# Two expert networks behind windowed attention: where the second sums accumulate, and when prepared weight slices are stored

## The chip, the cores and the metric

The kernel runs on one core of one Trainium2 chip. The metric is the device time of one execution in microseconds (us), as the median of several runs; less is better. TensorE (PE, with its weight loads as PEld) multiplies, VectorE (DVE) and ScalarE (ACT) do elementwise work, the queue of SyncE (SP) issues nearly all transfers, and the kernel's matmul results land in eight banks of PSUM.

## What is computed

The reference is attention over windows of chunks of 32 queries, with eight memory slots, followed by two feed-forward networks on 3072 tokens with 512 channels and 2048 hidden columns:

```python
for c in range(nc):                       # chunk 32, left 16, right 8, 8 memory slots
    a = softmax(scale * q_c @ k_full.T)   # k_full, v_full: memory and window
    out[:, :, c_start:c_end] = a @ v_full
x = out.transpose(0, 2, 1, 3).reshape(B * S, H * D)
r = np.maximum(x @ w_in1, 0.0)
x = (s * (r * r) + b) @ w_out1            # first network
h = x @ w_in2
out = (h * (1.0 / (1.0 + np.exp(-1.702 * h)))) @ w_out2   # second network
```

## The kernel before

**Arithmetic.** Each fp32 operand is split into a high and a low part (names ending in h and l), and each product of 128x128 by 128x512 is three matmuls: high by high, high by low, low by high. Tokens are cut into six blocks of 512. The hidden columns are cut into sixteen slices j of 128.

**Stages.** Attention of 24 tiles of 128 tokens runs beside the first network. Blocks 0 to 3 of the first network go through 66 units (`step`): a unit is one slice j for one block, four hidden sums into a bank of the ring `h`, four gate steps on ACT and DVE, and four output sums into `accA` and `accB` (two banks each). Each weight slice is loaded, taken apart on ACT and DVE (`words`, `prep`) in a ring `st` of three buffers and a ring `u` of four, and then stays in SBUF; all 32 are prepared in the first 150 us.

**Sweeps of seven products.** Blocks 4 and 5 of the first network, and then all six blocks of the second network in pairs, are done by `seven(s)`: for a pair of blocks (bp, bq) and a pair of slices, seven half-sized matrix products stand in for eight. A sweep takes eight steps p. The products accumulate in four places: A and C, one bank each of the ring `h` (two banks), B and D, the two banks of the tile `a`. DVE combines them in the SBUF tile `ys` (spots 0 to 3). The gates of block bp are used at once: `out_of(bp, ...)` adds them into `accA` (k = 0, 1) and `accB` (k = 2, 3) between the products; this is the first sum. The gates of block bq are stored to DRAM (`gd`), but for those of the last step, which stay in SBUF (`gq`). After step 7 and the last two `out_of(bp, ...)`, the sixteen `out_of(bq, ...)` follow; this is the second sum, 16 times 12 matmuls. It too accumulates in `accA` and `accB`, which `finish` has to copy out (`evac`, L223) first. Slices 14 and 15 come first from `gq`; the other fourteen are read back (`again`, L1136), the even ones into the ring `g`, the odd ones into the tile `back`, which takes the place of `ys`. During the second sum of the first sweep the output weights of the second network are also loaded (`reload`, L850), 512 KB a slice.

**The prepared slices.** `combine(p)` makes, for the sweep of the first network, the sums of weights that seven products need. Pieces that are plain copies are stored straight from the weight tiles (`keep`, L725: two stores of 256 KB and two of 128 KB for each p, 6.3 MB in all), as soon as the parts are there. The sums need DVE (`whole`, `sums`, `low`) and ACT (`high`), begin after the last weight is prepared, and are stored by L764. `pair` and `outer` do the like for the second network.

**Order.** Every operation is told to a planner (`Plan`) with its engine, an assumed duration, a due time and what it follows; `Plan.order` lists all of them by simulated time, and each engine executes its own list in that order, so an instruction that waits holds up what is listed behind it. Where the planner sees PE idle for over 0.3 us before the first output sum (`plan.first`), it fills in matmuls on a cold tile (`idle`, L1183), which write the bank of `accB`.

## Time and profile before

| what | us |
|---|---|
| median of three runs | 1110.62 |
| the three runs | 1107.44 to 1112.64 |
| the profiled execution | 1112.08 |
| its span, first to last instruction | 1110.2 |
| PE busy in the span | 1088.7 |
| DVE busy in the span | 711.0 |
| ACT busy in the span | 494.2 |

The page gives busy times by engine and by slices of the span; the windows give the same for chosen stretches, with the share of time in which the DMA engines were busy and the rate in GB/s. PEclk is the granted clock of TensorE as a share of full speed, and it is 1.00 all through. A timeline lists instructions in order of time, and in brackets the idle time before one and what ended it. The chain is the sequence of work that ended last, followed back from the end. The lines that the forecast rests on stand two sections below.

### The profile page before, as it was taken

How to read it: one execution, taken by the hardware profiler on the slowest of the kernel's cores; microseconds unless marked ns; L12 is line 12 of the kernel's file. 1: busy time of each engine (PE TensorE's matmuls, PEld its weight loads, DVE VectorE, ACT ScalarE, POOL GpSimd, SP SyncE). 2: the span in 40 equal slices, each digit the busy share in tenths (PEclk: the TensorE clock that was granted, in tenths of full speed). 3: DMA queues.
4: the chain of work that ended last, by engine and by line, in shares of the span. 5: the costliest groups of instructions: out<-in, count | busy, mean ns of one | idle time of the engine just before them, and what ended most of it. 6: DMA issues, size and time to landing. Idle time of an engine off the chain costs nothing.

```text
span 1110.2 us, 20092 instructions
## 1 busy us (share of the span) xinstructions
PE 1088.7 (98%) x7852; PEld 897.8 (81%) x7852; DVE 711.0 (64%) x1241; ACT 494.2 (45%) x842; POOL 0.7 (0%) x6
## 2 busy tenths in 40 slices
PE   8879999999999999999999999999999999999998
PEld 7768887888878788888888888888888888888886
DVE  6888988878778688687881455660555760655610
ACT  4678865555445455566640433330433430333310
POOL 0000000000000000000000000000000000000000
PEclk9999999999999999999999999999999999999999
DMA  8776627756678783888999965574755574654154
GB/s 326 245 258 209 208 105 248 259 193 219 208 275 267 265 301 117 312 294 279 318 323 382 322 203 200 183 260 144 246 188 201 202 246 155 203 190 142 76 191 150
DMA packets 119406, 252.99 MB, mean 228 GB/s; under 512 B 12816, under 2 KB 29200, under 8 KB 119312
## 3 DMA queue, kind: packets, MB, share of 16 engines
q1 hardware_dynamic: 119024, 251.19, 66.1%
q8 instruction: 62, 1.02, 0.4%
q10 hardware_dynamic: 288, 0.52, 0.1%
q14 instruction: 32, 0.26, 0.1%
HBM read 169.87 MB, written 81.79 MB: 227 GB/s over the span
## 4 chain that ended last, share of the span: by engine, by line
PE 92%; DMA 3%; DVE 2%; issue 1%; ACT 1%; SPq 0%; ACTq 0%; DVEq 0%
PE accA L1059 16%; PE accB L1059 16%; PE accA L640 7%; PE accB L640 7%; PE ph L981 5%; PE ph L983 5%; PE ph L982 5%; PE ph L602 5%; PE ph L603 5%; PE ph L604 5%; PE pb L983 4%; PE pb L981 4%; PE pb L982 4%; DMA st<-w_in 2%; PE o L479 1%; PE sc L418 1%
## 5 line engine op out<-in xcount | busy, mean ns | idle before, releaser
L997 ACT ACTIVATE r<-ys 128x512 f32<-128x512 f32 x72 | 45.5, 632 | 107.6 <-DVE ys L1094 81.2
L1083 DVE TENSOR_TENSOR ys<-pb,ys 128x512 f32<-128x512 f32 x32 | 22.0, 686 | 91.6 <-DMA out<-y 58.7
L602 PE MATMUL ph<-xh,wih 128*128 128x512 f32 (+1 forms) x200 | 79.3, 396 | 0.6 <-DVE xh L223 0.6
L603 PE MATMUL ph<-xl,wih 128*128 128x512 f32 (+1 forms) x200 | 76.6, 383 | 0.7 <-DVE xl L510 0.7
L604 PE MATMUL ph<-xh,wil 128*128 128x512 f32 (+1 forms) x200 | 76.4, 382 | 0.0
L223 ACT COPY y<-accA 128x512 f32<-128x512 f32 x20 | 10.9, 590 | 138.5 <-issue 84.4
L609 ACT ACTIVATE r<-ph 128x512 f32<-128x512 f32 (+1 forms) x66 | 38.5, 584 | 60.4 <-PE ph L604 54.2
L624 ACT CAST gh<-r 128x512 fp32r<-128x512 f32 (+1 forms) x66 | 40.2, 609 | 47.8 <-PE accB L640 31.2
L1094 DVE TENSOR_TENSOR ys<-pb,ys 128x512 f32<-128x512 f32 x32 | 22.1, 691 | 53.9 <-PE pb L983 53.3
L1006 DVE TENSOR_TENSOR r<-ph,r 128x512 f32<-128x512 f32 x24 | 16.6, 691 | 62.2 <-ACT r L997 62.2
L1059 PE MATMUL accA<-woh,gh 128*128 128x512 f32 x138 | 54.0, 391 | 0.0
L1059 PE MATMUL accA<-woh,gl 128*128 128x512 f32 x138 | 53.9, 390 | 0.0
L1059 PE MATMUL accB<-woh,gh 128*128 128x512 f32 x138 | 53.7, 389 | 0.0
L1059 PE MATMUL accA<-wol,gh 128*128 128x512 f32 x138 | 53.7, 389 | 0.0
L1059 PE MATMUL accB<-woh,gl 128*128 128x512 f32 x138 | 53.7, 389 | 0.0
L1059 PE MATMUL accB<-wol,gh 128*128 128x512 f32 x138 | 53.7, 389 | 0.0
L640 PE MATMUL accA<-gl,woh 128*128 128x512 f32 (+1 forms) x132 | 50.9, 385 | 2.2 <-DVE gl L628 2.2
L1019 ACT CAST gh<-r 128x512 fp32r<-128x512 f32 x64 | 39.8, 622 | 29.1 <-DVE r L1006 21.7
L342 ACT ACTIVATE st<-st 128x512 f32<-128x512 uint32 x64 | 42.8, 676 | 22.4 <-DMA st<-w_out 10.7
L640 PE MATMUL accA<-gh,woh 128*128 128x512 f32 (+1 forms) x132 | 51.4, 389 | 1.3 <-ACT gh L624 1.3
L640 PE MATMUL accB<-gl,woh 128*128 128x512 f32 (+1 forms) x132 | 50.6, 383 | 1.2 <-issue 1.2
L640 PE MATMUL accB<-gh,woh 128*128 128x512 f32 (+1 forms) x132 | 51.0, 387 | 0.0
(210 smaller groups left out, 2973.6 us busy)
## 6 DMA issues: line engine op xcount, KB each, us to landing
gd<-gq SPq DMA_DIRECT2D x56, 512.0 KB, 2.7
wih<-wch SPq DMA_DIRECT2D x96, 256.0 KB, 3.5
wil<-wcl SPq DMA_DIRECT2D x96, 256.0 KB, 3.8
st<-w_in SPq DMA_DIRECT2D x32, 512.0 KB, 5.4
st<-w_out SPq DMA_DIRECT2D x32, 512.0 KB, 5.0
back<-gd SPq DMA_DIRECT2D x56, 256.0 KB, 3.1
k<-k_w SPq DMA_DIRECT2D x24, 512.0 KB, 5.6
v<-v_w SPq DMA_DIRECT2D x24, 512.0 KB, 6.1
```

Source lines behind the costliest of these rows:

```text
L342: nc.scalar.activation(out=lo.bitcast(F32), in_=lo, func=AF.Copy, scale=2.0**-51, bias=2.0)
L602: nc.tensor.matmul(ph, wh, xh, start=(k == 0), stop=False)
L603: nc.tensor.matmul(ph, wh, xl, start=False, stop=False)
L604: nc.tensor.matmul(ph, wl, xh, start=False, stop=(k == KT - 1))
L624: nc.scalar.copy(out=T["g", i][0], in_=T["r", i])
L640: nc.tensor.matmul(o, lt, rh, start=fresh and x == 0, stop=(done and x == 2))
L981: nc.tensor.matmul(ph, wh, xh, start=first and i == 0, stop=False, skip_group_check=True)
L982: nc.tensor.matmul(ph, wh, xl, start=False, stop=False, skip_group_check=True)
L983: nc.tensor.matmul(ph, wl, xh, start=False, stop=i == 1, skip_group_check=True)
L997: nc.scalar.activation(out=T[rk], in_=src(), func=AF.Sigmoid, scale=GATE)
L1019: nc.scalar.copy(out=T[key][0], in_=T[rk])
L1059: nc.tensor.matmul(a, lt, rh, start=n == 0 and x == 0, stop=n == NF - 1 and x == 2)
```

## The change

Four things are changed, all in the lists given to the planner.

1. `keep`, the stores of prepared slices, now also follow the last output sum of unit 16 + p (`end_`), where they followed the preparation of the slice alone.
2. In `combine`, the second whole slice (`wb`) is written into the last half of the `st` buffer that later holds the sums, and no longer into a `u` buffer. The number of DVE and ACT operations is the same.
3. In the last step of the first network's sweep the gates of block bq work in place in their spot of `ys` (`there`), and no longer in a `u` buffer.
4. The second sum accumulates in the banks of the seven products: k = 0, 1 in the tile `a`, k = 2 and k = 3 in one bank of the ring `h` each, in the order k = 2, 3, 0, 1. `accA` and `accB` are left to the first sum. The tile `a` is opened only by a product B or D, and `plan.first` becomes the first four output sums, of which the earliest start counts.

```diff
-                idle = min(starts[i], starts[self.first]) - clock
+                idle = min(starts[i], *(starts[x] for x in self.first)) - clock
...
-            if plan.first is None:
-                plan.first = d
+            if len(plan.first) < KT:
+                plan.first.append(d)
...
+        o_unit[i] = d
...
-            acc = T["acc", group, k // 2][:, k % 2]
+            acc = T[held] if len(T[held].shape) == 2 else T[held][:, k % 2]
...
-        done = [op(need, {"sp": 0.75}, keep(v, w0, slice(0, 512), slice(0, 2)), after=first[v:v + 1], uses=[w0]) for v in range(2)]
+        end_ = [o_unit[16 + p]]
+        done = [op(need, {"sp": 0.75}, keep(v, w0, slice(0, 512), slice(0, 2)), after=first[v:v + 1] + end_, uses=[w0]) for v in range(2)]
...
-                T[k, p] = stp.tile([P, 512], F32, tag="u", name="u", bufs=4)
+                if k == "wa":
+                    x = T[k, p] = stp.tile([P, 512], F32, tag="u", name="u", bufs=4)
+                else:
+                    T["s", p] = stp.tile([P, 4, 256], F32R, tag="st", name="st")
+                    x = T["s", p].bitcast(F32)[:, 2:4].rearrange("p n d -> p (n d)")
...
-                if ("pb", s) not in T:
+                if c in "BD" and ("pb", s) not in T:
...
+            there = not (mine or away or m)
+
             def gate1(e):
-                T[rk] = (gp if mine else stp).tile([P, 512], F32, tag="r" if mine else "u", name="r", bufs=1 if mine else 4)
+                T[rk] = src() if there else (gp if mine else stp).tile(
+                    [P, 512], F32, tag="r" if mine else "u", name="r", bufs=1 if mine else 4)
...
+            here_r = uses if there else [rk]
...
+            second = b == bq
+            place = [("a", ("acc", group, 0)), ("a", ("acc", group, 0)), ("h", ("acc", group, 2)), ("h", ("acc", group, 3))] if second else [
+                (halves[k // 2], ("acc", group, k // 2)) for k in range(KT)]
+            for k in (2, 3, 0, 1) if second else range(KT):
+                tag, acc = place[k]
+                opens = n == 0 and (tag == "h" or k % 2 == 0)
```

## Rows read from the trace of the kernel before

**Rows 1.** The page, its first part: busy us, share of the span, instructions.

```profile
PE 1088.7 (98%) x7852; PEld 897.8 (81%) x7852; DVE 711.0 (64%) x1241; ACT 494.2 (45%) x842; POOL 0.7 (0%) x6
```

**Rows 2.** Windows by stage: stretch, length, busy us (instructions), PEclk, DMA share, GB/s.

```profile
0.00:35.00 35.00, 29.70 (x692) 27.79 (x693) 24.18 (x50) 17.50 (x30) 0.70 (x6) 1.00 0.88 309
35.00:80.00 45.00, 37.58 (x691) 30.93 (x689) 37.45 (x68) 32.77 (x60) 0.00 (x0) 1.00 0.80 271
...
296.00:312.00 16.00, 14.10 (x309) 11.17 (x308) 11.88 (x22) 7.61 (x12) 0.00 (x0) 1.00 0.72 249
...
364.00:380.00 16.00, 15.27 (x195) 12.38 (x194) 8.61 (x16) 6.57 (x10) 0.00 (x0) 1.00 0.89 297
...
612.00:776.00 164.00, 163.71 (x719) 134.49 (x718) 82.92 (x132) 52.92 (x89) 0.00 (x0) 1.00 0.65 219
```

**Rows 3.** Timeline of PE: start us, us, line, operation, idle before and what ended it.

```profile
46.02 0.39 PE L640 MATMUL accA<-gh,woh 128*128 128x256 f32 x1 [1.28 <-ACT gh L624]
...
311.78 1.09 PE L493 MATMUL xx<-ident,px 128*128 128x128 f32 x8 [1.88 <-DVE px L484]
```

**Rows 4.** Timeline of the SP queue, 13 to 37 us: start us, issue us, line, transfer.

```profile
13.48 0.33 SPq L725 DMA_DIRECT2D wch<-wih  x1
14.98 0.88 SPq L403 DMA_DIRECT2D qe<-q_t  x2
...
18.22 0.38 SPq L725 DMA_DIRECT2D wcl<-wil  x1
...
36.89 0.33 SPq L326 DMA_DIRECT2D st<-w_in  x1
```

**Rows 5.** Timeline of PE, 141 to 143 us, the last output sum of unit 16.

```profile
142.12 0.39 PE L640 MATMUL accB<-gh,wol 128*128 128x512 f32 x1
```

**Rows 6.** Windows of 10 us behind the preparation of the weights, columns as in rows 2.

```profile
150.00:160.00 10.00, 10.00 (x45) 8.28 (x45) 8.51 (x17) 5.46 (x10) 0.00 (x0) 1.00 0.08 26
...
180.00:190.00 10.00, 10.00 (x165) 7.83 (x164) 9.43 (x17) 4.50 (x7) 0.00 (x0) 1.00 0.82 264
```

**Rows 7.** The SP queue's own waits: line, what it waited for, us, times, longest.

```profile
SPq L725 <- ACT wzh L223: 16.7, 4, 9.0
```

**Rows 8.** The chain that ended last, 295 to 375 us: start us, us, piece.

```profile
300.75 8.73 DMA st<-w_in
```

**Rows 9.** The chain, 728 to 745 us, first to second sum of the second sweep.

```profile
733.83 1.47 PE accA L1059 x6
735.29 1.40 PE accB L1059 x6
...
742.25 1.36 PE accA L1059 x6
```

**Rows 10.** Timeline of ACT at the end of that second sum.

```profile
776.33 1.07 ACT L223 COPY y<-accA 128x512 f32<-128x512 f32 x2 [28.86 <-issue]
```

**Rows 11.** Timeline of PE at the start of the second sweep.

```profile
615.99 0.50 PE L981 MATMUL ph<-xs,wih 128*128 128x512 f32 x1 [0.29 <-ACT ys L1081]
```

**Rows 12.** Timeline of the SP queue, 562 to 581 us, the first reads of `back`.

```profile
563.05 1.74 SPq L1136 DMA_DIRECT2D back<-gd  x4
```

**Rows 13.** Timeline of DVE, 564 to 570 us, the last gate of the first sweep.

```profile
568.07 0.68 DVE L1022 TENSOR_TENSOR gq<-r,gq 128x512 fp32r<-128x512 f32 x1
```

**Rows 14.** Windows over the second sum of the first sweep, columns as in rows 2.

```profile
560.00:568.00 8.00, 8.00 (x37) 6.63 (x36) 7.27 (x14) 5.82 (x11) 0.00 (x0) 1.00 0.82 280
568.00:576.00 8.00, 7.90 (x35) 6.19 (x34) 5.22 (x10) 1.17 (x2) 0.00 (x0) 1.00 0.95 326
...
588.00:612.00 24.00, 24.00 (x107) 19.68 (x106) 0.27 (x1) 0.00 (x0) 0.00 (x0) 1.00 1.05 386
...
624.00:628.00 4.00, 4.00 (x20) 3.30 (x19) 3.53 (x6) 2.23 (x4) 0.00 (x0) 1.00 1.05 394
```

**Rows 15.** Waits of the weight loads after 440 us: line, releaser, us, times, longest.

```profile
PEld accA L1059 <- DMA back<-gd: 0.3, 1, 0.3
```

**Rows 16.** Timeline of PE, 587 to 598 us, a product of the second sweep among the sums.

```profile
596.49 0.39 PE L981 MATMUL ph<-xh,wih 128*128 128x512 f32 x1
```

More of the change, by code (lines that the diff above doesn't have):

```diff
@@ L217, in attention_moe_moe @@
     plan = Plan()
-    plan.first = None
+    plan.first = []
     op = plan.op
@@ L673, in step, with finish @@
                 finish(m, b, k, group, lo, hi, d, at_o[i] + 4)
+        o_unit[i] = d
     o_store = {}
-    def finish(m, b, k, group, lo, hi, after, need):
+    def finish(m, b, k, group, lo, hi, after, need, at=None):
         part, more = hi < NF, lo > 0
+        held = at or ("acc", group, k // 2)
         def evac(e):
-            acc = T["acc", group, k // 2][:, k % 2]
+            acc = T[held] if len(T[held].shape) == 2 else T[held][:, k % 2]
             if part:
@@ L699, in store @@
             nc.sync.dma_start(out=dst, in_=T["y", m, b, k])
[L701 removed]
+        acc = held
         if part:
@@ L728, in combine @@
         first = list(o_w[w0]) + list(o_w[w1])
-        done = [op(need, {"sp": 0.75}, keep(v, w0, slice(0, 512), slice(0, 2)), after=first[v:v + 1], uses=[w0]) for v in range(2)]
-        done += [op(need, {"sp": 0.4}, keep(v, w1, slice(256, 512), slice(2, 3)), after=first[2 + v:3 + v], uses=[w1]) for v in range(2)]
+        end_ = [o_unit[16 + p]]
+        done = [op(need, {"sp": 0.75}, keep(v, w0, slice(0, 512), slice(0, 2)), after=first[v:v + 1] + end_, uses=[w0]) for v in range(2)]
+        done += [op(need, {"sp": 0.4}, keep(v, w1, slice(256, 512), slice(2, 3)), after=first[2 + v:3 + v] + end_, uses=[w1])
+                 for v in range(2)]
         def whole(w, k):
             def fn(e):
-                T[k, p] = stp.tile([P, 512], F32, tag="u", name="u", bufs=4)
+                if k == "wa":
[3 more added lines that the diff above has]
+                    x = T["s", p].bitcast(F32)[:, 2:4].rearrange("p n d -> p (n d)")
                 h, l = T[w]
-                nc.vector.tensor_tensor(out=T[k, p], in0=h.bitcast(F32), in1=l.bitcast(F32), op=ALU.add)
+                nc.vector.tensor_tensor(out=x, in0=h.bitcast(F32), in1=l.bitcast(F32), op=ALU.add)
             return fn
@@ L758, in combine @@
         a = op(need, {"dve": 0.65}, whole(w0, "wa"), after=first[:2] + end_, alloc=[("u", ("wa", p))], uses=[w0])
-        b = op(need, {"dve": 0.65}, whole(w1, "wb"), after=first[2:] + end_, alloc=[("u", ("wb", p))], uses=[w1])
-        c = op(need, {"dve": 1.5}, sums, after=[a, b], alloc=[("st", ("s", p))], uses=[("wa", p), ("wb", p)])
+        b = op(need, {"dve": 0.65}, whole(w1, "wb"), after=first[2:] + end_, alloc=[("st", ("s", p))], uses=[w1])
+        c = op(need, {"dve": 1.5}, sums, after=[a, b], uses=[("wa", p), ("s", p)])
         h = op(need, {"act": 1.05}, high, after=[c], alloc=[("st", ("sh", p))], uses=[("s", p)])
@@ L1022, in gate4 @@
                 nc.vector.tensor_tensor(out=T[key][1], in0=T[rk], in1=T[key][0].bitcast(F32), op=ALU.subtract)
-            a = op(need, {"act": 0.6}, gate1, after=d, alloc=[("r" if mine else "u", rk)], uses=uses)
+            a = op(need, {"act": 0.6}, gate1, after=d, alloc=[] if there else [("r" if mine else "u", rk)], uses=uses)
+            here_r = uses if there else [rk]
             last = a
@@ L1037, in gates @@
             own = [] if mine else [box]
-            g1 = op(need, {"act": 0.62}, gate3, after=[b], alloc=here, uses=[rk] + own, **kw)
-            g2 = op(need, {"dve": 0.66}, gate4, after=[g1], uses=[rk] + own)
+            g1 = op(need, {"act": 0.62}, gate3, after=[b], alloc=here, uses=here_r + own, **kw)
+            g2 = op(need, {"dve": 0.66}, gate4, after=[g1], uses=here_r + own)
             if not mine and away:
@@ L1048, in out_of, with fn @@
             own = [box] if key == ("g", s, j, False) else list(over)
-            for k in range(KT):
-                def fn(e, k=k):
-                    if n == 0 and k % 2 == 0:
-                        T["acc", group, k // 2] = ps_acc.tile([P, 2, 512], F32, tag=halves[k // 2], name=halves[k // 2])
-                    a = T["acc", group, k // 2][:, k % 2]
+            second = b == bq
[4 more added lines that the diff above has]
+                opens = n == 0 and (tag == "h" or k % 2 == 0)
+                def fn(e, k=k, tag=tag, acc=acc, opens=opens):
+                    if opens:
+                        if tag == "h":
+                            T[acc] = ps_h.tile([P, 512], F32, tag="h", name="ph")
+                        else:
+                            T[acc] = (ps_a if second else ps_acc).tile([P, 2, 512], F32, tag=tag, name="pb" if second else tag)
+                    a = T[acc] if tag == "h" else T[acc][:, k % 2]
                     wh, wl = T[wout]
```

22 lines of the change are left out of this document (10 added, 12 removed).

## The prediction, made before the changed kernel was run

> **What bounds the kernel now.** I read the page first. PE is busy for 98% of the span [rows 1], so only PE's idle time, its dummy matmuls and the tail can be won; no arithmetic is removed. The windows by stage say where that idle time lies [rows 2]. In the first 35 us PE is idle for 5.3 us and in the next 45 for 7.4, while DMA is busy 0.88 and 0.80 of the time. Behind that it is nearly full: 1.9 us are lost between 296 and 312, 0.7 between 364 and 380, and a whole sweep of seven products loses 0.3 of 164 us. All that this change can give the four sweeps is therefore small, and the early stretch decides. The reader should see that the words of the change speak of the sweeps' banks, while the idle time is elsewhere.
>
> Next I took the timeline of PE. The early waits end on the last step of a gate or of attention, on ACT or DVE [rows 3]; behind these stands DVE work on a late load, as at 36.89, where a weight load is issued behind other transfers [rows 4], and in the chain at 300.75, where a load takes 8.73 us [rows 8]. The engines' lists are fixed by a planner that expects loads earlier than this, so a late load holds up DVE, and behind it PE: 1.88 us at 311.78 [rows 3].
>
> **The stores put off.** They are 32 transfers on the SP queue, four for each p, and the first goes out at 13.48 us [rows 4]. The new condition, the end of units 16 to 23, comes from 142 us on, one unit apart [rows 5], by my count of the units' last sums (the eighth is near 184). 256 KB at the 386 GB/s of the fullest stretch [rows 14] take 0.68 us of DMA. Ahead of the loads up to 36.89 stand three times 256 KB, at 13.48 and 18.22 [rows 4] and as two halves at 28.6 to 29.0, and a fourth in the next 15 us: 4 x 0.68 = 2.7 us if each lies on the chain. From the other side, a new list can add a stall of the size of the largest one seen, 1.88 us and the 0.4 of a refilled pipeline, so +2.3. I take two of the four, since the store at 13.48 is right ahead of the q loads and the pair at 28.6 is ahead of the load at 36.89, whose delay ends in the 1.28 us before 46.02 [rows 3]; the others lie before transfers that have slack: **-1.3** (between -2.7 and +2.3). The planner will also lay out the early lists anew; the trace cannot show that order, and the bounds stand for it.
>
> Where they go, DMA has room: between 150 and 160 its share is 0.08, and PE is full [rows 6]. All of them need 6.3 MB / 386 GB/s = 16 us, and about 23 us are free in the five windows of 10 us from 140 to 190, two of which stand in rows 6. But the last of them has a share of 0.82 already, and DVE is busy 0.94 of it [rows 6]. The new wait stands on the SP queue, on PE's unit. Behind it queue the stores of the sums, which free the `st` buffers that DVE and ACT want next, the loads of attention for block 2, and y1 stores. Before, the same line held the queue for up to 9.0 us without a loss on PE [rows 7]. So I take **+0.2**, between 0 and +2.3, again one stall.
>
> The two later stretches with stalls lose 1.9 and 0.7 us, 2.6 in all [rows 2]. The stores are gone by then on either side, but the list may shift: **0**, between -2.6 and +2.6. The second whole slice in an `st` buffer keeps all counts; its DVE add of 0.7 us now waits for a store that frees the buffer, one operation earlier than the sums did. It is in the +0.2.
>
> **The second sums' banks.** From the second sweep on, the step from first to second sum costs PE 1.47 against 1.36 us for the first block of six matmuls and 1.40, 1.40, 1.40 and 1.39 for the next [rows 9]: 0.11 + 3 x 0.04 + 0.03 = 0.26 us, and three sweeps have it. With the banks of the products free since the last gates, this goes: 3 x -0.26 = -0.8. What is late next is the other end: product B of the next sweep needs the tile `a`, whose k = 1 is now the last sum of all. ACT copies a pair of banks in 1.07 us, waiting for both [rows 10], and A, six matmuls, covers 1.36 [rows 9]. The margin is 0.29, less two signals; I put +0.1 on each of three, +0.3, bounded by 0 and 3 x 0.5. Together **-0.5**, between -0.8 and +0.7.
>
> **The first sweep's second sum** is another case, because there DMA is full: 0.95 from 568 to 576, over 1.0 from 588 to 612, with 386 GB/s [rows 14]. Each slice of 2.72 us on PE brings 512 KB of read-back and 512 KB of `reload`, 4 x 0.68 = 2.7 us. The loads come just in time; PE waits once for `back` [rows 15]. Two things change. First, the gates in place hold `ys` until the last gate ends at 568.75 [rows 13], and `back` takes the place of `ys`. Its first four loads, issued at 563.05 [rows 12], move to about 569. They need 2.7 us; of the 8 us that they enter 0.05 are free [rows 14], which is 0.4 us. So the queue is up to 2.3 us later from there on. Second, at 596.49 PE took a product A of the next sweep in between [rows 16], which gave the loads 1.36 us; now A needs a bank of `h` that holds a sum, and cannot be drawn ahead. Walking through it: PE waits some 2.3 us more for read-backs, pays A behind the sum instead of inside it, and drops its own PSUM wait of the size above (0.26) and the one at 615.99 (0.29 and the refill [rows 11]). That is +1.9; if the queue absorbs the four loads it is -0.9. With all of it in sequence, +2.7. I take **+1.2**, nearer to the former, since the windows show the queue full.
>
> One rule speaks against that. The Trainium skill's page "DMA: Bandwidth & Descriptors", section "Measured", gives 425 GB/s for a core that streams alone. An estimate from it: 1.05 MB in 2.47 us, 0.25 us a slice to spare, so 2.3 us would be caught up in nine slices, and the term would be -0.9 and the sum -2.5. The trace does not agree so far: no stretch that I read passes 394 GB/s [rows 14].
>
> The gates in place keep their operations, and the tail (last copy, store) keeps its order.
>
> **Sum.** -1.3 + 0.2 + 0 - 0.5 + 1.2 = -0.4 us. On the profiled execution's 1112.08 that is 1111.7; that execution is 1.5 above the median of the runs, so on the median of 1110.62 it is **1110.2**. A difference under 0.5% (5.6 us) cannot be told from none with this kernel: the three runs before span 5.2.
>
> **The rivals.**
> - *The early stretch is bound by transfers*. Then freeing DMA gives more than the bytes in front of two loads: half of the 12.7 us of idle in the first 80 [rows 2], 6.4 instead of 1.3, so 1110.2 - 5.1 = 1105.1, and with the smaller of the later stalls gone as well 1104.4. For it: the DMA shares of 0.88 and 0.80. Against: loads wait for buffers, and DVE is busy for 37 of the 45 us behind 35 [rows 2]. Chance 0.12.
> - *The queue of the first sweep catches up*. The four late loads fit, the read-backs are in time, the term is -0.9: 1110.2 - 2.1 = 1108.1. For it: reload has slack. Against: 386 GB/s at a share of 1.05 [rows 14]. The page above stands behind this case. Chance 0.20.
> - *The banks bring nothing, as loads set the pace*. The first sweep's term is +2.7 and the next sweeps' starts lose what their middles gain, +0.5 for -0.5: 1110.2 + 1.5 + 1.0 = 1112.7. Chance 0.13.
> - *SP is held by the new wait, and DVE behind it* (slower). Each p has stores that wait for PE's unit; if the planner lists them ahead of the stores that free `st`, DVE stands still with its 0.94 load [rows 6], and the gates of the units come late. From the point where a hold exceeds the slack of a unit, about 5.4 - 3 = 2.4 us, it reaches PE; three of eight at 2.0 (a stall as at 311.78) add 6 us: 1116. For it: in-order queues and no spare DVE. Against: 9.0 us of the like were harmless [rows 7]. Chance 0.09.
>
> **How the numbers follow.** The forecast has 0.46: 1107.5 to 1113, no change that can be told. The second and third rivals stay inside 0.5% as well. The range leaves out the slower rival and takes in the first: 1104 to 1115, with the bounds of the early lists on both sides. Faster by over 0.5% is the first rival and a little of the bounds, 0.13; slower is the last and a little, 0.10; within 0.5%, 0.77.
>
> **What would show it.** In the trace after: no store of L725 before 140 us; idle of PE in 0 to 80 down by one or two us from 12.7; blocks of six matmuls at 1.36 right behind the first sums; no product of a next sweep before the last sum; reads of `back` from 568.7 on and PE waits on them between 580 and 600. I am wrong if PE's idle time in the first 80 us changes by over 3 us either way, if new waits on `st` show between 142 and 230, or if the loads of the second sum stay in time.

## The result, and the profile of the changed kernel

The changed kernel takes 1117.59 us (median of 20 runs, 1111.86 to 1126.14), the kernel before 1110.26 in the runs beside it (20 runs, 1107.10 to 1112.64). The ratio is 1.0068, with an interval of 1.0051 to 1.0085: **slower by 0.7%**, where 1110.2 within 1104 to 1115 was forecast. The profiled execution of the changed kernel took 1116.73 us.

First the page of the changed kernel and its windows by stage, which answer to [rows 1, 2]. Columns as there: stretch, length, busy us of PE, PEld, DVE, ACT and POOL (instructions), granted clock, DMA share, GB/s.

```profile
PE 1093.2 (98%) x7840; PEld 900.5 (81%) x7840; DVE 712.0 (64%) x1250; ACT 490.5 (44%) x833; POOL 0.7 (0%) x6
```

```profile
0.00:35.00 35.00, 30.41 (x678) 28.36 (x679) 22.26 (x46) 15.56 (x27) 0.70 (x6) 0.95 0.73 262
35.00:80.00 45.00, 40.44 (x703) 34.38 (x702) 38.88 (x71) 32.24 (x59) 0.00 (x0) 0.96 0.72 244
142.00:230.00 88.00, 88.00 (x889) 72.64 (x888) 73.58 (x129) 46.89 (x75) 0.00 (x0) 1.00 0.74 255
...
448.00:612.00 164.00, 157.50 (x673) 126.69 (x673) 119.05 (x221) 83.17 (x146) 0.00 (x0) 0.99 0.89 313
612.00:776.00 164.00, 164.00 (x721) 134.85 (x720) 82.93 (x132) 53.12 (x89) 0.00 (x0) 1.00 0.68 235
```

The early stretch has less idle time (9.2 us in the first 80 against 12.7; part of that is the granted clock, 0.95 and 0.96 here, at which PE is busy for longer with the same work). The stretch with the stores is full, the second sweep is full. All the loss stands in one row: the first sweep, 448 to 612. The kernel before had 163.90 of the 164 us there:

```profile
448.00:612.00 164.00, 163.90 (x720) 134.61 (x719) 114.59 (x209) 80.97 (x142) 0.00 (x0) 1.00 0.91 321
```

To compare executions I cut them at three matmuls: the start of the first sum (L1080; L1059 before), the start of the second sum, and the last matmul. The first piece holds all of attention and the units, the second the first sum of the first sweep, the third the rest. Against a second execution of the kernel before (1109.40 us, below) the changed one is 2.2 us quicker in the first piece (456.0 against 458.2), 4.2 slower in the second (112.49 against 108.26) and 5.1 slower in the third (541.50 against 536.38): 7.1 of the 7.3 us between them. The first piece scatters between executions (more on that with unit 8 below); the other two carry the loss.

**The second piece: one stall at 500 us.** Timelines of SP, ACT, DVE and PE of the changed kernel (start us, us, line, operation, idle before and what ended it):

```profile
492.39 1.45 SPq L326 DMA_DIRECT2D st<-w_in  x2
```

```profile
500.78 0.66 ACT L332 ACTIVATE u<-st 128x512 f32<-128x512 f32 x1 [3.50 <-DMA st<-w_in]
```

```profile
501.47 0.43 DVE L338 TENSOR_SCALAR u<-u 128x512 f32<-128x512 f32 x1 [3.50 <-ACT u L332]
501.81 0.68 DVE L1122 TENSOR_TENSOR ys<-pb,ys 128x512 f32<-128x512 f32 x1
```

```profile
502.55 0.50 PE L988 MATMUL pb<-xl,wih 128*128 128x512 f32 x1 [2.59 <-DVE ys L1122]
```

It is read upwards. PE waits for DVE to empty a bank (L1122). DVE's next instruction was L338, a step that prepares a slice of the *second* network's weights, which nobody needs yet; it waits for ACT's L332, and that for a load issued at 492.39 that lands 8.4 us later. L1122 stood behind it in DVE's list. The matmul before this one started at 499.57, so PE started nothing for 2.98 us, 2.75 more than the usual 0.23. The stall costs more than that, as the granted clock shows behind it:

```profile
502.00:503.00 1.00, 0.45 (x2) 0.41 (x3) 1.00 (x3) 1.00 (x3) 0.00 (x0) 1.00 1.04 395
503.00:504.00 1.00, 1.00 (x5) 0.80 (x4) 1.00 (x4) 0.69 (x2) 0.00 (x0) 0.66 0.60 213
504.00:505.00 1.00, 1.00 (x3) 0.79 (x3) 0.99 (x3) 1.00 (x3) 0.00 (x0) 0.50 0.19 70
...
507.00:508.00 1.00, 1.00 (x6) 0.83 (x5) 1.00 (x3) 0.61 (x2) 0.00 (x0) 1.00 0.89 356
```

At 0.50 (1.2 GHz) a matmul starts every 0.43 us instead of 0.23; eight of them make 1.6 us, and 2.75 + 1.6 accounts for the 4.2 us of this piece.

**The third piece: the second sum waits for its loads.** Timeline of PE, then the waits of PE and its weight loads from 580 to 612 (line, releaser, us, times, longest), then the windows that answer to [rows 14]:

```profile
588.17 1.14 PE L1080 MATMUL ph<-back,woh 128*128 128x512 f32 x2 [0.32 <-DMA back<-gd]
...
593.06 0.50 PE L1080 MATMUL ph<-gh,woh 128*128 128x512 f32 x1 [1.47 <-DMA gh<-gd]
```

```profile
PEld ph L1080 <- DMA gh<-gd: 2.7, 2, 1.9
PEld ph L1080 <- DMA back<-gd: 2.5, 4, 0.8
...
PEld ph L1080 <- DMA gl<-gd: 1.0, 2, 0.5
```

```profile
560.00:568.00 8.00, 8.00 (x37) 6.64 (x36) 7.93 (x15) 6.04 (x11) 0.00 (x0) 1.00 0.52 184
568.00:576.00 8.00, 8.00 (x37) 6.53 (x36) 7.46 (x17) 1.52 (x3) 0.00 (x0) 1.00 0.93 316
588.00:612.00 24.00, 20.89 (x83) 15.32 (x84) 7.57 (x14) 1.36 (x2) 0.00 (x0) 1.00 1.04 392
```

Before, PE waited once for `back`, 0.3 us [rows 15]; now four pairs of waits from 588 to 610 add up to 5.0 us, counted from start to start of the matmuls. DMA is as full as before, but DVE is now busy for 7.6 us between 588 and 612 where it had 0.27 [rows 14]: work has come into this stretch that was not there. The list of SP's transfers tells which (line, transfer, count: issue ns min/median/max, first and last start us), before and after:

```profile
L806 SPq DMA_DIRECT2D wcl<-st x32: 319/380/1816, 223.0 to 550.0; - x32
```

```profile
L813 SPq DMA_DIRECT2D wcl<-st x32: 319/382/997, 230.7 to 582.1; - x32
```

These are the stores of the second network's prepared slices (`pair`). They begin 8 us later and end 32 us later. The last eight, those of pair 7, went out by 550 before the change, ahead of the second sum; now they go out from 570.9 to 582.1, in the middle of it, with two loads of `w_out` (586.8, 598.4) and the last two stores of `wod` (601.9, 613.1).

### The profile page after: what moved, and what is told of

The parts are those of the page before. It is cut to its first block, busy times and chain, and to the rows that moved or that the text cites. A ratio compares the mean times of both kernels' runs of the same rounds, so it can differ in the third digit from the quotient of the medians.

```text
span 1114.8 us, 20017 instructions
## 1 busy us (share of the span) xinstructions
PE 1093.2 (98%) x7840; PEld 900.5 (81%) x7840; DVE 712.0 (64%) x1250; ACT 490.5 (44%) x833; POOL 0.7 (0%) x6
## 2 busy tenths in 40 slices
DMA packets 119405, 252.97 MB, mean 227 GB/s; under 512 B 12816, under 2 KB 29200, under 8 KB 119312
## 4 chain that ended last, share of the span: by engine, by line
PE 83%; DMA 8%; DVE 6%; issue 1%; ACT 1%; SPq 1%; ACTq 0%; DVEq 0%
PE accA L1080 8%; PE accB L1080 7%; PE ph L1080 6%; PE pb L1080 6%; PE accA L640 6%; PE accB L640 6%; PE ph L988 5%; PE ph L990 5%; PE ph L989 5%; PE ph L602 4%; PE ph L603 4%; PE ph L604 4%; PE pb L988 4%; PE pb L990 4%; PE pb L989 4%; DMA st<-w_in 2%
## 5 line engine op out<-in xcount | busy, mean ns | idle before, releaser
L988 PE MATMUL pb<-xl,wih 128*128 128x512 f32 x128 | 50.7, 396 | 3.2 <-DVE ys L1122 3.2
L223 ACT COPY y<-ph 128x512 f32<-128x512 f32 x8 | 4.7, 588 | 106.2 <-issue 54.4
L640 PE MATMUL accA<-gh,wol 128*128 128x512 f32 (+1 forms) x132 | 50.7, 384 | 0.2 <-DVE wol L312 0.2
L640 PE MATMUL accB<-gh,wol 128*128 128x512 f32 (+1 forms) x132 | 50.5, 383 | 0.0
L1007 ACT ACTIVATE r<-ph 128x512 f32<-128x512 f32 x24 | 14.3, 597 | 82.1 <-PE ph L990 82.1
L988 PE MATMUL ph<-xh,wih 128*128 128x512 f32 x128 | 50.3, 393 | 0.0
L990 PE MATMUL pb<-xl,wil 128*128 128x512 f32 x128 | 50.2, 392 | 0.0
```

The costliest lines, as they stand in the source:

```text
L640: nc.tensor.matmul(o, lt, rh, start=fresh and x == 0, stop=(done and x == 2))
L988: nc.tensor.matmul(ph, wh, xh, start=first and i == 0, stop=False, skip_group_check=True)
L990: nc.tensor.matmul(ph, wl, xh, start=False, stop=i == 1, skip_group_check=True)
L1007: nc.scalar.activation(out=T[rk], in_=src(), func=AF.Sigmoid, scale=GATE)
```

## The experiments

Two theories at the start. **Theory 1**: the stores put off make the planner lay out the second network's preparation later, and that preparation costs the time, by its transfers and by standing in front of the sweep's own work. **Theory 2**, the prediction's: the reads of `back` held by the gates in place, and the missing product A, make the second sum late. Later a third came up: any list laid out anew loses time somewhere.

All runs at a glance. "To second sum" and "rest" are the second and third piece of above; "last store" is that of pair 7; PE is its busy time of the 164 us from 448 to 612.

| kernel | ratio to before, interval | median us | first sum starts | to second sum | rest | last store | PE |
|---|---|---|---|---|---|---|---|
| before (shown) | | 1110.6 | 460.6 | 108.3 | 536.5 | 550.0 | 163.90 |
| before again (one run) | | 1109.4 | 458.2 | 108.3 | 536.4 | 547.6 | 163.90 |
| **after** | 1.0068 [1.0051, 1.0085] | 1117.6 | 456.0 | 112.5 | 541.5 | 582.1 | 157.50 |
| after again | 1.0064 [1.0040, 1.0087] | 1116.7 | 456.5 | 108.9 | 542.3 | 579.1 | 158.92 |
| stores put off, alone | 1.0073 [1.0048, 1.0097] | 1117.4 | 452.3 | 117.9 | 538.3 | 567.3 | 154.90 |
| after, stores undone | 1.0010 [0.9997, 1.0024] | 1111.1 | 455.3 | 108.6 | 538.1 | 545.3 | 162.81 |
| after, banks undone | 1.0073 [1.0052, 1.0094] | 1117.5 | 456.2 | 113.5 | 539.5 | 575.4 | 157.40 |
| after, half of reload | 1.0020 [0.9998, 1.0041] | 1111.5 | 457.1 | 112.2 | 537.9 | 582.2 | 160.35 |
| after, pair 7 not stored | 1.0010 [0.9991, 1.0030] | 1110.9 | 456.6 | 110.8 | 537.0 | none | 161.15 |
| stores, unit 8 | 0.9954 [0.9935, 0.9973] | 1104.5 | 453.6 | 108.4 | 536.5 | 543.2 | 163.61 |
| stores, unit 12 | 1.0061 [1.0040, 1.0082] | 1115.7 | 452.0 | 117.4 | 539.1 | 566.4 | 154.89 |
| after, unit 8 | 0.9978 [0.9965, 0.9991] | 1107.2 | 455.0 | 108.5 | 537.7 | 544.8 | 163.14 |
| stores, unit 8, and banks | 0.9941 [0.9922, 0.9959] | 1103.7 | 452.6 | 108.0 | 536.8 | 542.1 | 163.62 |
| gates in place, alone | 1.0004 [0.9986, 1.0022] | 1110.0 | 454.5 | 109.4 | 537.0 | 545.1 | 162.78 |
| after, pairs 6, 7 due early | 1.0099 [1.0083, 1.0115] | 1119.8 | 467.5 | 108.3 | 535.9 | 550.3 | 163.96 |
| before, pair 7 late | 1.0116 [1.0089, 1.0143] | 1122.4 | 460.7 | 117.7 | 539.3 | 575.4 | 154.73 |
| after, pairs 6, 7 early | 1.0035 [1.0010, 1.0061] | 1114.1 | 456.7 | 114.8 | 536.8 | 557.4 | 159.67 |
| after, pairs 4 to 7 early | 0.9991 [0.9972, 1.0010] | 1108.9 | 453.2 | 108.6 | 536.5 | 541.0 | 163.77 |

### Which part

Stores put off alone, on the kernel before:

```diff
+        end_ = [o_unit[16 + p]]
-        done = [op(need, {"sp": 0.75}, keep(...), after=first[v:v + 1], uses=[w0]) ...]
+        done = [op(need, {"sp": 0.75}, keep(...), after=first[v:v + 1] + end_, uses=[w0]) ...]
```

> Only the stores of prepared slices are put off; banks, gates and combine are as before. Theory: putting the stores off makes the planner lay out new lists, in which the early stretch is shorter (first output sum of the sweeps at 456 us instead of 460.6), but the second network's weight preparation ends later (last store of a prepared output slice at 600 to 613 us instead of 580.5), and its transfers fall into the first sweep's second sum, where DMA is full. So that second sum to the second sweep's third product takes 50 to 52 us instead of 47.1, and the whole 1112 to 1118. Rival (the banks and the gates in place hold up the read-backs): without them that stretch takes 47, the early gain stays, and the whole is 1106 to 1108.

Part one undone in the changed kernel (the same lines the other way; the second whole slice stays in the `st` buffer, as changed):

> The changed kernel with the stores of prepared slices at their old place; banks, gates in place and the st buffer as changed. Theory: lists as before up to the first sweep's end, preparation ends at 580; the stretch from the second sum to the third product of the second sweep takes 46.5 to 49 us, the whole 1109.5 to 1112.5, and the spread of the runs is that of before. Rival (banks and gates cause the loss): that stretch takes 52 us as in the changed kernel, the whole 1115.

The banks undone in the changed kernel:

```diff
-            second = b == bq
+            second = False
```

> The changed kernel with the second sums back in accA and accB, so that a product of the next sweep can again be drawn ahead; stores put off and gates in place stay. Theory: the preparation is still late, the second sum still waits for read-backs: that stretch takes 50 to 52 us, the whole 1114 to 1118. Rival (the product that cannot be drawn ahead is the price): the stretch falls to 48 to 49 us and the whole to 1111 to 1113.

The changed kernel once more, unaltered:

> The changed kernel once more, for a second profile. Theory: the waits between 588 and 610 us recur within 1 us in sum, since bytes set them; the one at 502 us hangs on one late load and may be there or not, and with it the fall of the granted clock behind it; 1112 to 1122 in single runs. Rival (all waits are fixed by the lists): the same waits at the same places to 0.3 us, and the spread has another cause.

The stores alone lose all of it (1.0073), and without them the other three parts are at 1.0010. So the loss is part one's. But it does not sit at the same place. With the stores alone PE loses 9.2 us in one piece, at the start of the second sum. Timelines of PE and ACT of that kernel:

```profile
570.13 1.52 PE L1077 MATMUL accA<-gq,woh 128*128 128x512 f32 x2 [9.03 <-ACT gq L1026]
```

```profile
562.29 0.63 ACT L1009 ACTIVATE r<-r 128x512 f32<-128x512 f32 x1
566.22 0.40 ACT L223 CAST st<-u 128x256 fp32r<-128x256 f32 x1 [3.30 <-DMA wcl<-st]
566.53 0.61 ACT L1026 CAST gq<-r 128x512 fp32r<-128x512 f32 x1
```

The last gates (L1026) stand behind a cast of pair 7 (L223, `st<-u`), which waits for a store to free its buffer; DVE has thirteen instructions of pair 7 in front of its own step of the gate. With the banks undone the loss moves once more: at 569.69 PE waits 3.87 us for ACT to copy out `accA`, since two steps that prepare pair 7 (at 567.42 and 568.75, each behind DVE) stand in front of that copy in ACT's list; the waits for read-backs are gone, and the time is the same (1.0073).

In the second execution of the changed kernel the stall at 501 us is 0.6 us long and the clock does not fall, while the waits in the second sum come again (5.7 us): the former varies, the latter doesn't. Timeline of PE there:

```profile
500.92 0.50 PE L988 MATMUL pb<-xl,wih 128*128 128x512 f32 x1 [0.46 <-DVE ys L1122]
```

Theory 2's parts cost 1.7 us (538.1 against 536.4) and not 5.

### What in the second sum

The loads of `reload` halved (256 KB a slice instead of 512; the low half is replaced by the high one):

```diff
-            T[w] = weight_tiles("wo")
-            for v in range(2):
-                nc.sync.dma_start(out=T[w][v].bitcast(F32), in_=wod[j][:, v])
+            t = wp.tile([P, 512], F32R, tag="woh", name="woh", bufs=plan.tags["wo"][0])
+            T[w] = [t, t]
+            nc.sync.dma_start(out=t.bitcast(F32), in_=wod[j][:, 0])
```

> The kernel after with the loads of `reload` cut to their high half (256 KB instead of 512 KB for a slice; the low half is replaced by the high one, so the second network's sums use the high weights twice). The order of all lists is that of after. Theory 1 (the transfers of pair 7's preparation do not fit into the second sum of the first sweep, which is full of read-back and reload): 16 x 256 KB = 4.2 MB less, over 10 us of DMA; the waits of PE between 585 and 612 go, the stretch from the begin of the second sum to the third product of the next sweep takes 47 to 48.5 us instead of 52.1 to 52.9, and the time falls by 3 to 5 us, to 1112 to 1114. Theory 2 (the waits come from where instructions stand on SP, ACT or DVE, not from bytes): the stretch stays at 51.5 to 53 and the time within 1 us of after.

Pair 7's stores and the last two of `wod` left out:

```diff
             def store(v):
+                if p == NF // 2 - 1:
+                    return lambda e: None
...
-        o_wod[j] = op(need, {"sp": 1.45}, lambda e: nc.sync.dma_start(...), after=[a], uses=[key])
+        o_wod[j] = op(need, {"sp": 1.45}, lambda e: None if j > NF - 3 else nc.sync.dma_start(...), after=[a], uses=[key])
...
```

> The kernel after without the eight stores of pair 7's prepared slices and the two stores of the last two prepared w_out slices (2.84 MB); the loads that would read them read the slices before. All other instructions and the order are those of after. Theory 1 (these bytes, issued between 570 and 613, are what the second sum lacks): the stretch from the begin of the second sum to the third product of the next sweep takes 47 to 48.5 us instead of 52.1 to 52.9, and the time is 1112 to 1113.5, 3 to 5 us under after. Theory 2 (not these bytes but the order of the instructions, or the reads of `back` alone): 51.5 to 53, and 1115.5 to 1117.5. If only the reads of `back`, late by the gates in place, counted, the kernel without the stores put off would have shown the same waits; it showed under 2 us.

The rest falls from 541.5 and 542.3 to 537.9 and to 537.0, against 536.4 before: 3.6 to 5.3 us come back, with every list in the order of the changed kernel. So the waits of the second sum are **a matter of bytes**: the halved loads take nothing else away. The 2.88 MB of late stores (252.97 MB moved in all, 250.09 without them) are enough to make them, though leaving stores out also frees their buffers sooner. By the ratios the two are 5 and 6 us under the changed kernel. The runs spread widely (1102.5 to 1116.5 in the latter); the stall at 502 us is still there, 2.4 and 1.8 us in the two profiles.

### How far the stores are put off

Units 8 to 15 instead of 16 to 23, banks and gates as before (this and unit 12 have the second whole slice in `st`, as in the change):

```diff
-        end_ = [o_unit[16 + p]]
+        end_ = [o_unit[8 + p]]
```

> Part one alone in a milder form: the stores of the prepared slices wait for units 8 to 15 instead of 16 to 23, half a pass of the units sooner; banks and gates as in the kernel before. Theory 1 (the loss is the second network's preparation running late, not the wait as such): if the last stores of pair 7 come out near 550 as in the kernel before, the stretch to the second sum is 108 to 109 and the second sum with the two products 47 to 49; the time is that of before within 3 us, 1107 to 1113. Rival (any wait on a unit in SP's queue costs, by what it holds up behind it): the loss stays, 1114 to 1117, and PE's idle time lies between 100 and 230.

The kernel before again, for its profile:

> The kernel before once more, for its profile alone: how much do the stretches of one and the same kernel differ between two executions? The profile shown of before ended its stretch up to the first sums at 460.6, the kernels after at 455.3 to 456.5, and one of these still had the stores in their old place. If that gain belongs to the change, this one ends it at 460 to 461; if it is the scatter of executions, it ends anywhere between 455 and 461. From there on it should show 108.3 to the second sum and 47.1 to the third product in either case.

Units 12 to 19:

> As the kernel with unit 8 alone, with units 12 to 19: a point between units 8 to 15 (1104.5) and units 16 to 23 (1117.4). Theory 1 (the later the stores, the later the preparation): the last stores of pair 7 lie between those two, about 555 to 575, and the time between, 1107 to 1115; the later the last stores, the larger the waits of PE between 500 and 610. Rival (the lists are laid out by chance, and any of them can fall well or ill whatever the number of units): the lateness and the time don't follow the number: under 1105 or over 1117.

The changed kernel whole, with unit 8:

> The kernel after with one number changed: the stores put off wait for units 8 to 15 instead of 16 to 23. Theory 1 (the whole loss of the change is the preparation that runs late because the stores go out so late; the rest of the change costs what the kernel without the stores put off showed, 1.7 us in the second sum of the first sweep): the last store of pair 7 is issued before 550, the waits of PE between 585 and 610 are under 2 us together, and the time is 1105 to 1107.5, one to two us above the kernel with unit 8 alone. Rival (the parts only work together, the banks and the gates in place being what fills the second sum): the waits of 5 us stay there, and the time is 1109 to 1112.

Unit 8 **gains** 0.46% (0.27% to 0.65%), below both ranges expected; unit 12 loses 0.61%, unit 16 0.73%. Unit 16 alone has the second whole slice in a `u` buffer; in the whole change, where the unit is the only difference, 16 is at 1.0068 and 8 at 0.9978. What part two by itself does to the gain, no run shows. With unit 8 the preparation ends at 543.2, and what follows the start of the first sum is as long as before (108.4 + 536.5 against 108.3 + 536.4). So its gain, 5.1 us by the ratio and 4.5 by the medians, lies ahead of that point, most of it in the early stretch (the 150th matmul of the units' output sums starts at 112.0 against 115.3 in the second execution of the kernel before). Windows of unit 8 and of the second execution of before:

```profile
0.00:80.00 80.00, 72.53 (x1390) 63.70 (x1391) 63.37 (x120) 49.85 (x89) 0.70 (x6) 0.98 0.73 254
```

```profile
0.00:80.00 80.00, 69.74 (x1392) 61.13 (x1393) 65.73 (x124) 51.34 (x91) 0.70 (x6) 1.00 0.85 290
```

The DMA share falls from 0.85 to 0.73 and PE's idle time from 10.3 to 7.5 us. Single executions scatter here. Four have the lists of the kernel before as far as the first sum (that kernel twice, and below the gates in place alone and pair 7 late): they start it at 460.6, 458.2, 454.5 and 460.7. Six with the lists of the changed kernel start it at 456.0 to 457.1, three with unit 8 at 452.6 to 455.0. The means are 458.5, 456.5 and 453.8: the order holds, and a gain read from one pair of profiles does not.

Unit 12 has the 9 us wait for the last gates, as the stores alone had it with unit 16:

```profile
569.39 1.52 PE L1080 MATMUL accA<-gq,woh 128*128 128x512 f32 x2 [9.11 <-ACT gq L1029]
```

Its time is a little over the 1107 to 1115 that theory 1 gave it: the time follows the last store, but by a step and not a slope. The kernels so far with the last store by 550 lose at most 2.0 us behind the start of the first sum; those at 566 to 582, with all their transfers, are 6 to 8 us over the kernel before. The whole change with unit 8 is at 0.9978.

### The other parts by themselves

Unit 8 with the banks (the changed kernel at unit 8 with `there = False`), and the gates in place alone on the kernel before:

```diff
+            there = not (mine or away or m)
...
-                T[rk] = (gp if mine else stp).tile([P, 512], F32, tag="r" if mine else "u", name="r", bufs=1 if mine else 4)
+                T[rk] = src() if there else (gp if mine else stp).tile(
+                    [P, 512], F32, tag="r" if mine else "u", name="r", bufs=1 if mine else 4)
...
```

> The kernel with unit 8 and the banks of the second sums, without the gates in place. It parts the 1.7 us that the second sum of the first sweep took longer with banks and gates together (48.8 against 47.1). Theory 1, that of the prediction's term: both have a share, the reads of `back` late by the gates in place and no product A drawn ahead by the banks; then this kernel shows 47.8 to 48.3 there. Theory 2: the reads alone; then 46.8 to 47.2, the three later transitions gain their 0.26 each and lose part of it at the next product B, and the time is that of the kernel with unit 8 alone within 1 us, 1103.5 to 1105.5.

> The kernel before with the last gates in place and nothing else. If the gates alone make the 1.7 us (the first reads of `back` some 4 us later while the transfers are full), the stretch from the second sum's begin to the third product is 48.5 to 49 instead of 47.0, with PE waits on `back`, gh or gl between 578 and 592, and the time is 1110.5 to 1112. If the second sum absorbs four late reads, it is 47.0 to 47.3, and the time is that of before within 1 us.

On the rest the banks cost 0.3 us (536.8 against 536.5 with unit 8 alone), the gates 0.6 (537.0 against 536.4), both 1.2 with unit 8 and 1.7 with the stores in their old place. The stretch that the expectations name, from the second sum's begin to the third product, takes 47.1 with the gates alone, 47.4 with the banks and 48.3 with both at unit 8, against 47.1 and 47.0 in the kernel before: the second sum absorbs the four late reads, and only the two parts together cost a microsecond.

In the medians one difference can be told. With unit 8 and the banks, the gates in place cost 3.6 us (1107.23 against 1103.67, and the intervals of the ratios do not meet: 0.9965 to 0.9991, 0.9922 to 0.9959). The profiles show 1.3 us of that behind the start of the first sum; 2.4 lie ahead of it, where both kernels have the same lists. Where the rest comes from stays open. Stores at unit 8 with the banks is the fastest kernel of the study, 1103.67 us, 0.9941.

### Is the late preparation the cause?

So far it only went along with the loss. Four kernels move it. First, the changed kernel with due times for pairs 6 and 7:

```diff
+        n = len(plan.ops)
...
+        for i in range(n, len(plan.ops)):
+            if p in {6:470,7:510}:
+                plan.due[i] = {6:470,7:510}[p]
```

> The kernel after, stores put off to units 16 to 23 as there, but the preparation of the second network's pairs 6 and 7 is given due times (470 and 510 in the planner's count), so that the lists take it up about as early as in the kernel before. Nothing else is changed. Theory 1 (the loss is that preparation being late, not the late stores as such): pair 7's last store is issued near 550 instead of 582, no wait of over 1 us at 500 or 570 is left, the second sum with what follows loses 1 to 2 us instead of 5, as in the kernel without the stores put off, and the time is 1107 to 1112. Rival (the late stores themselves, or the lists around them, cost the time; the preparation only moves with them): 1115 to 1118, or the waits go and as much idle time of PE comes up elsewhere, above all between 230 and 450.

Then the kernel before with pair 7's three groups of loads bound to later sums, for the planner:

```diff
+    for i, d in ((1957, 2337), (1989, 2435), (1999, 2465)):
+        plan.ops[i][3].append(d)
```

> The counter-test, on the kernel before: the stores stay in their old place and all lists are the same until the loads for pair 7, which the planner may set only behind sums of the first sweep that it places at 525, 554 and 575; by its lists pair 7's last store comes at 578 or so instead of 550 and the last prepared w_out slice at 610 instead of 580. Theory 1: this alone makes the loss, PE waits 4 us or more between 500 and 612 (in front of the last gates at 565 to 570, or in the second sum), and the time is 1113 to 1119. Rival: 1108 to 1111.5, and PE is as full between 448 and 612 as in the kernel before.

The second is plain: the lists stay those of the kernel before to 523 us, and it loses 13.7 us, more than the change does and more than was expected. The 9 us wait for the last gates is there, and behind it the clock at half, as the timeline of PE and the windows show:

```profile
578.44 1.52 PE L1059 MATMUL accA<-gq,woh 128*128 128x512 f32 x2 [9.21 <-ACT gq L1019]
```

```profile
578.00:580.00 2.00, 1.56 (x3) 1.03 (x4) 0.69 (x1) 0.97 (x2) 0.00 (x0) 0.50 1.01 274
580.00:582.00 2.00, 2.00 (x6) 1.52 (x6) 0.00 (x0) 0.00 (x0) 0.00 (x0) 0.50 0.89 326
582.00:584.00 2.00, 2.00 (x6) 1.54 (x5) 0.00 (x0) 0.00 (x0) 0.00 (x0) 0.50 1.08 383
584.00:586.00 2.00, 2.00 (x9) 1.62 (x8) 0.00 (x0) 0.00 (x0) 0.00 (x0) 0.83 1.00 381
```

The first went half as expected: the first sweep is full (163.96 of 164), no wait is left in the second sum, and yet the kernel is the slowest but one, because the planner hands a due time on to what stands before, and the lists from 142 to 230 came out differently:

```profile
142.00:230.00 88.00, 75.91 (x1058) 62.35 (x1057) 68.91 (x116) 39.27 (x61) 0.00 (x0) 0.88 0.74 259
```

There the chain runs through a store that frees an `st` buffer and an addition that waits for it (the second whole slice, which part two moved into `st`), in front of attention's steps on DVE (start us, us, piece); from 190 to 210 the granted clock is 0.50:

```profile
184.27 5.69 DMA wcl<-st
...
189.99 0.70 DVE st L744
```

So the same due times were set again, for these operations alone and not handed on:

```diff
+        for i, t in self.force.items():
+            late[i] = t
...
+        for i in range(n, len(plan.ops)):
+            if p in {6:470,7:510}:
+                plan.force[i] = {6:470,7:510}[p]
```

> The kernel after with all lists the same until some 495 us; from there on the operations that prepare pairs 6 and 7 of the second network are taken up as early as their inputs and buffers allow (a due time set for them alone, not handed on to what stands before them, as in the former run, where the early lists moved as well and lost 12 us between 142 and 230). Theory 1: pair 7's last store is issued near 555 instead of 582, there is no wait over 1 us near 500 or 570, PE is nearly as full between 448 and 612 as in the kernel before, 162 of 164 us or more, and the time is 1108 to 1112.5, the early gain of the stores put off less the 1 to 2 us of banks and gates. Rival (the lateness is not what costs): 1115 or more.

> As the former run, with pairs 4 to 7 taken up early instead of 6 and 7: the lists are those of after until some 390 us. In the former run the 5 us of waits in the second sum were gone, but the stall at 502 us (2.0 us) stayed, behind loads of pair 6 that were still issued at 493 as in after (475 in the kernel before). Theory 1 (that stall too is the late preparation): pair 6's loads come near 475 to 480, the stall at 502 is gone, 448 to 612 has 162.5 us or more of PE, and the time is 1107 to 1111.5 with a narrower spread than the 14 us of the former run. Rival (that stall has another cause, in the early or middle lists of after): it stays or another of 2 us takes its place, and the time is 1113 to 1117.

With pairs 6 and 7 the waits of the second sum go (536.8 instead of 541.5) and half the time comes back, 1114.1, between what theory 1 and its rival had expected. A stall at 502 us stays, behind loads of pair 6 that are still issued at 493.0, and PE waits for the last gates for 1.05 us at 568 and 0.58 at 572, which theory 1 did not expect:

```profile
502.47 0.50 PE L992 MATMUL pb<-xl,wih 128*128 128x512 f32 x1 [1.85 <-DVE ys L1126]
```

With pairs 4 to 7 these loads come at 473.7, of these waits 0.2 us is left, and the time is that of the kernel before, 0.9991, with all parts of the change in place and the stores still at units 16 to 23. Windows of that kernel:

```profile
448.00:612.00 164.00, 163.77 (x716) 133.67 (x715) 113.41 (x212) 80.90 (x142) 0.00 (x0) 1.00 0.94 333
```

Taken away, the late preparation takes the loss with it; made by itself, it makes the loss. Theory 1 is shown, and in two ways: as steps that stand in front of the sweep's own in an engine's list, and as transfers. The third theory is not empty: one of the lists laid out anew lost 12 us elsewhere.

What stays open: why the planner's lists let 8 us at pair 0 grow to 32 at pair 7, and why the changed kernel with its preparation mended stays 0.37% above the kernel with unit 8 alone (the whole change with unit 8 lies between; the gates in place, told above, may be a part of it). Its runs spread from 1104.8 to 1113.5, those of unit 8 from 1103.1 to 1105.2. The rows from 448 us on are alike in the two profiles (163.77 and 163.61), which speaks for a difference ahead of that; no run here parts it further.

## Why the prediction was wrong, point by point

**The later lists, 0 between -2.6 and +2.6: the step that failed.** The bound was made from the idle time of the two stretches that already had stalls [rows 2]. A full stretch was taken to stay full. But the change moves 32 transfers in a list that a planner lays out, and what it fills in last, the preparation, has no due time of its own near its place. The row that would have told it was to be had: pair 7's last store at 550.0 in the kernel before, 19 us ahead of the second sum, in a stretch with DMA at 0.91. A delay of 20 us there meets both the last gates and a full queue. In the changed kernel's two executions the term measured +4.2 and +0.7 us at 500, and some 4 of the 5 to 6 us in the second sum. And the prediction counted no fall of the granted clock behind a stall, 1.6 us of the +4.2.

**The stores put off, -1.3 (-2.7 to +2.3).** The sign was right. In the changed kernel the first sum starts 2.0 us earlier by the means above, within the bounds. With unit 8, where nothing is lost behind, the gain is 0.46% or about -5 (-7 to -3), the first rival's size (-5.1) and outside the bounds. The share of DMA over the whole early stretch, which that rival used, may have been the better row; how much of the gain is transfers that were freed and how much the new lists is not shown. The sign "idle time in the first 80 us changes by over 3 us" came: 3.5 us less, and between the second executions of both kernels 3.4, with the clock at 1.00 in both:

```profile
0.00:80.00 80.00, 73.11 (x1401) 64.33 (x1402) 65.26 (x123) 51.81 (x92) 0.70 (x6) 1.00 0.73 258
```

**The new wait, +0.2.** The number held (88.00 of 88 us are full from 142 to 230, and 86.86 in the second execution, against 87.72 before), the picture was wrong. The stores wait for no unit of PE: `after` is a condition for the planner's order, and no signal stands for it. The SP queue's own waits from 130 to 190 have one on this line:

```profile
SPq L727 <- DMA wcl<-wil: 0.2, 1, 0.2
```

The first of these stores is issued at 136.89 (forecast: none before 140), ahead of the last matmul of unit 16's sums, which starts at 137.34.

**The fourth rival, the slower one (0.09).** Its place was wrong, 142 to 230, and so was its first half, SP held by the new wait. Its second half is what happened: an engine that works its list in order stands before a step that waits for a transfer, and the gate behind it is late. It happened at 502 in the changed kernel and at 570 in those with the stores alone, behind loads and stores of the preparation; at 142 to 230 it came only in the kernel with due times handed on. That its 1116 lies near the 1117.6 measured is luck.

**The second sums' banks, -0.5 (-0.8 to +0.7).** Nothing gained: from one first sum to the next, sweeps 2 to 4, it is 164.15 us against 164.10. The chain of the second sweep, answering to [rows 9], shows why:

```profile
737.06 1.36 PE accB L1080 x6
738.42 1.40 PE ph L1080 x6
739.82 1.40 PE pb L1080 x6
...
783.49 0.35 PE pb L988
```

The first block's 1.47 is 1.40 now, but the blocks behind it still take 1.40: these 0.04 were counted as part of the bank's wait, and they are not. Product B of the next sweep waits 0.12 us, as forecast.

**The first sweep's second sum, +1.2 (-0.9 to +2.7).** As the price of these two parts it was well sized: +1.7 without the stores put off, +1.2 with unit 8, 0.1 with pairs 4 to 7 early. Its working has a slip: 2.3 - 0.26 - 0.29 and 0.4 for the refill come to 1.35, not 1.9. The four reads were issued from 566.89 instead of 563.05 [rows 12], and no product was drawn ahead. In the changed kernel the term is +5, beyond the bound, since transfers came into the queue that the walk through it had not counted.

**The second rival, that the queue catches up (0.20)**, had a condition that the kernels without late stores come near to: the read-backs are in time. Its -0.9 was not reached; nearest is the kernel with due times handed on, whose rest is 535.9 against 536.4. The Trainium skill's page "DMA: Bandwidth & Descriptors", section "Measured", gives 425 GB/s for one core alone. Here that rate is passed in single moments (438 from 500 to 501 in the kernel before) but not held: 386 from 588 to 612 there [rows 14], 392 in the changed kernel, 398 in its fullest 24 us (606 to 630).

**The third rival, that loads set the pace (0.13)**, had the direction of the first sweep's term right and its size, +2.7, too small; the later sweeps, together +0.5 in it, cost 0.05 each.

## What to carry to other kernels

Where lists are laid out by a planner, an edit's cost lies not only where its instructions stand: ask what the planner fills in last, and how far that is from the next stretch in which an engine's list or the transfers have no room. A bound for "the list may shift" cannot be taken from today's stalls; a stretch at 100% is the one that a shift can hurt. And a step put off should be put off as little as brings the gain: put off by eight units the stores gained 5 us, by sixteen they lost 8.

## What the runs showed of the hardware

A single gap of PE could cost more than its length. Behind the gap at 500 us in the changed kernel (PE started nothing for 3.0 us) the granted clock stood at 0.50 for some 3 us, and behind the 9 us gap of the kernel before with pair 7 late for about 6; at the same place it fell to 0.50 behind 2.6 us (half of `reload`) and 2.2 us (pairs 6 and 7 early) as well. Behind 2.0 us there (pair 7 not stored), and between the waits from 588 to 610, in which PE started nothing for up to 1.9 us, it stayed at 1.00. Half the clock made 1.6 us of the loss in the first case, and in the second most of the 2.9 us by which the rest was longer.
